# Attention on fp32 operands with one turn on TensorE, in front of two feed-forward layers: a new attention part of a fused kernel

## The chip, the cores and the metric

One Trainium2 chip, of which the kernel uses one core. The metric is the device time of one execution in microseconds (us); the kernel before takes 700.09 us (median of three executions). Engine names are those of the profile: PE is TensorE's matmul, PEld its weight load, DVE is VectorE, ACT is ScalarE, POOL is GpSimd, and SP issues nearly all transfers.

## The reference

An attention with a small learned bias on the relative position, and behind it two feed-forward layers on 1152 tokens (2 batches of 576). The feed-forward weights come as 64-bit floats and are converted on the chip.

```python
B, H, S, D = 2, 8, 576, 64
scores = np.matmul(q, k.transpose(0, 1, 3, 2)) / np.sqrt(D)
x = (log1p(abs(i - j)) / log1p(max(i, 1)))[..., None]       # one value for each pair of positions
bias = np.maximum(x @ w1 + b1, 0.0) @ w2                    # 32 hidden units, 8 heads
attn = softmax(scores + bias)                               # 1e-9 is added to each row's sum
x = np.matmul(attn, v)                                      # to (1152, 512)
x = g1(x @ moe_w_in) @ moe_w_out                            # g1(h) = h * clip(h + 3, 0, 6) / 6, 2048 hidden
out = g2(x @ moe2_w_in) @ moe2_w_out                        # g2(h) = P(h) / Q(h), a cubic over a quadratic
```

## The kernel before

The program has two parts. The **attention part** runs first, and its work is written as a list of small steps (`plan`), which are issued in the order of a table of numbers (`ORDER`). Each engine executes its own instructions strictly in that order, so the table sets both what an engine does next and what it is stuck behind. The **dense part** is a loop over 96 units of the two feed-forward layers: each unit is a matmul group `h` of 12 matmuls over 384 tokens, an elementwise chain, and a matmul group `y`; three units of the first layer are already issued inside the attention part.

The attention part works on five chunks of queries (`qc` 0 to 4): four chunks of 128 positions, each for both batches (`b` 0 and 1), and a last chunk that holds the remaining 64 positions of both. A pair of heads (`hp`) is handled together, one head on each half of the 128 partitions. A "unit" `u` is one chunk and one head, so there are 40 units, and for each unit and batch there are these steps:

- **bias**: 36 groups (`G`), eight for each of the first four chunks and four for the last. A group is four hidden-unit tiles (`bias_unit`, L528 on DVE or L526 on ACT), eight small matmuls that sum over hidden units on four column tiles of the array (`bias_sums`, L535), a scaled copy to SBUF on ACT (`bias_scaled`, L542) and a transfer that lays the rows out by position (`bias_out`, L551). `huge` holds the bias of a chunk, and there are two such buffers.
- **splitting q, k and v**: each is multiplied by a power of two and split into two fp16 parts, high and low. The power comes from sums of squares that PE takes (`gram`, L472, 128-column fp32 matmuls), that DVE turns into an exponent (L476 to L505). ACT writes the high parts (L577, L588, L597), DVE or POOL the low parts (L570, L572, L573).
- **scores**: 16 fp16 matmuls for a pair, four products of high and low parts, one head on each half of the array's rows (L613, L628 for the last chunk). They write two of the three two-bank PSUM buffers of `ps2`.
- **logits**: one DVE instruction that adds the bias and finds the row's extreme (`logits`, L636), and one that reads the accumulator. **exp** on ACT (L917).
- **turning the exponentials** so that keys lie on partitions. For 24 of the 40 units (`BY_DMA`): ACT writes a high fp16 part (L926), POOL the low part (L931), and a DMA transpose turns both (L938). For the other 16: PE turns three 128x128 blocks at a time into one PSUM bank (L950, 40 such pieces), ACT writes the high part (L957) and DVE the low part (L963). All those pieces, and the turning of the results, use one and the same bank (`pst`).
- **product with v**: 15 fp16 matmuls of 65 columns for each unit and batch (L650). The 65th column of v is ones and gives the row's sum. DVE divides (L658 to L663), PE turns the result (L670), ACT and DVE split it for the dense part (L679, L680).

SP's queue holds the loads, the bias transfers and the DMA transposes, in the table's order as well. The dense part's weights arrive as 64-bit words; DVE converts them (L213 to L215), ACT and POOL split them (L241, L242). Six of the 64 weight tiles are loaded and converted inside the attention part.

Of the kernel before, what the change touches and what calls it, by code (L numbers as in the profile page):

```python
# [10 lines left out]
F32 = mybir.dt.float32  # L11
F32R = mybir.dt.float32r
# [21 lines left out]
EXP_SHIFT = 14  # L34
E23 = float(1 << 23)
# [4 lines left out]
PRODUCTS = ((0, 0), (0, 1), (1, 0), (1, 1))  # L40
V_DVE = (0, 1, 2, 4, 7)
UNSCALED = (0, 1, 2, 3)
U_ENG = ((0, 1, 0, 1) + (0, 1, 0, 0)) * 4 + ((0, 0, 1, 0) + (0, 1, 0, 0)) * 14
BY_DMA = (1, 2, 3, 4, 6, 7, 8, 9, 11, 12, 13, 14)
PTX = (1,) * 20 + (0,) * 20
N_W = 6
M_AT = ((33.5, 34, 38.1), (34.5, 35, 38.3), (35.5, 36, 38.6))
N_EARLY = 3
ORDER = (
# [56 lines left out]
def _constants():  # L106
# [7 lines left out]
    rps = (1.0 / psi_i.astype(np.float64)).astype(np.float32)[rows[:, p // NH].T]  # L114
    msk = (np.arange(32)[None, :] // NH == (p // HID)[:, None]).astype(np.float32)
    small = np.concatenate([psq, rps, msk, np.eye(P, dtype=np.float32)], axis=1).astype(np.float32)
    return {"cpsi": psi.astype(np.float32), "csmall": np.ascontiguousarray(small)}


def _rows(ap, parts, n):  # L120
# [1017 lines left out]
```

## Time and profile before

| what | value |
|---|---|
| median of 3 executions | 700.09 us (699.69 to 701.59) |
| span of the profiled execution, first to last instruction | 698.0 us |
| PE busy in the span | 617.2 us (88%) |
| DVE busy | 522.5 us (75%) |
| ACT busy | 415.8 us (60%) |
| POOL busy | 284.8 us (41%) |

The profiled execution's own time is its span plus what lies around it; the median above lies 2.1 us over this span. Busy time is the union of the instructions' times on an engine. A matmul's row lasts until its modelled end, and the next one starts long before that, so the cost of a row of matmuls is read from start to start. An fp32 matmul leaves two records in the trace, a turn and an fp16 matmul one.

### The profile page before, as it was taken

Reading aid. Unit: us, or ns where it says so; the run is one execution under the profiler, and the core shown is the slowest. Engines: PE = TensorE matmul, PEld = TensorE weight load, DVE = VectorE, ACT = ScalarE, POOL = GpSimd, SP = SyncE. Lnnn points to the kernel's source line nnn. Section 1 sums busy time; section 2 is a strip of 40 time slices with the busy share of each in tenths; the row PEclk is TensorE's granted clock in tenths of the full one; section 3 lists DMA queues with packets and bytes.
Section 4 is the critical chain, followed back from the end, with each engine's and each line's share of the span. In section 5 each row is a group of like instructions: output and inputs, shape, how many; then the busy total and the mean of one; then the engine's idle time right before and its main releaser. Section 6 shows DMA issues by size and latency. Waiting matters only on the chain.

```text
span 698.0 us, 12904 instructions
## 1 busy us (share of the span) xinstructions
PE 617.2 (88%) x5022; PEld 524.7 (75%) x5022; DVE 522.5 (75%) x1027; ACT 415.8 (60%) x723; POOL 284.8 (41%) x248
## 2 busy tenths in 40 slices
PE   9777988687875969799899999998899789999997
PEld 8454644254553758799899999998799679999985
DVE  6558878876796852999977847989977887666674
ACT  5747786696766443454333333356788677777863
POOL 1114654363346400334323214127456855455543
PEclk9979999899997999899999999999999999999999
DMA  6655765379768403635434600333411000000011
GB/s 241 132 190 128 155 127 131 85 171 187 152 164 213 84 1 109 193 122 181 151 122 131 228 5 30 91 92 104 137 31 31 1 1 0 1 1 0 1 76 60
DMA packets 88012, 70.87 MB, mean 102 GB/s; under 512 B 58512, under 2 KB 75024, under 8 KB 87952
## 3 DMA queue, kind: packets, MB, share of 16 engines
q1 hardware_dynamic: 87952, 70.06, 36.9%
q8 instruction: 39, 0.64, 0.4%
q14 instruction: 21, 0.17, 0.1%
HBM read 41.73 MB, written 2.36 MB: 63 GB/s over the span
## 4 chain that ended last, share of the span: by engine, by line
PE 55%; DVE 19%; issue 9%; DMA 6%; POOL 5%; ACT 5%; SPq 0%; DVEq 0%; POOLq 0%; ACTq 0%
PE y L372 21%; PE h L289 21%; DVE wk L215 3%; PE h L472 3%; PE ps L535 3%; DVE big L528 3%; DVE wk L214 3%; DVE wk L213 3%; DMA huge<-wk 2%; DMA xt<-big 2%; PE ps L613 2%; PE h L950 2%; PE h L650 2%; POOL big L931 2%; DVE big L636 2%
## 5 line engine op out<-in xcount | busy, mean ns | idle before, releaser
L289 PE MATMUL h<-xt,huge 128*128 128x384 f32 x504 | 102.4, 348 | 6.7 <-DVE gl L314 2.1
L289 PEld LDWEIGHTS h<-xt,huge 128*128 128x128 f32 x504 | 93.0, 196 | 10.7 <-DVE gl L314 2.8
L324 POOL TENSOR_TENSOR e<-e,e 128x384 f32<-128x384 f32 x48 | 51.1, 1066 | 64.3 <-ACT e L322 62.5
L931 POOL TENSOR_TENSOR big<-big,big 128x1152 f16<-128x1152 f32 x24 | 58.7, 2450 | 41.4 <-ACT big L926 40.3
L636 DVE CUSTOM_DVE_ANT_0 big<-ps,huge,nscale 128x576 f32<-128x576 f32 (+1 forms) x72 | 57.3, 819 | 20.9 <-PE ps L613 10.8
L289 PE MATMUL h<-xt,big 128*128 128x384 f32 x324 | 63.2, 343 | 5.4 <-DVE e L336 5.4
L289 PEld LDWEIGHTS h<-xt,big 128*128 128x128 f32 x324 | 58.2, 192 | 7.0 <-DVE e L336 6.3
L314 POOL TENSOR_TENSOR gl<-e,gh 128x384 fp32r<-128x384 f32 x48 | 50.1, 1048 | 31.8 <-ACT gh L313 23.9
L613 PE MATMUL ps<-kT,qT 64*128 64x512 f16 (+1 forms) x512 | 45.3, 306 | 19.9 <-DVE mx L636 12.8
L917 ACT ACTIVATE big<-big,mx 128x576 f32<-128x576 f32 (+1 forms) x72 | 53.6, 772 | 13.8 <-DVE mx L636 7.8
L242 POOL TENSOR_TENSOR huge<-wk,huge 128x512 fp32r<-128x512 f32 x28 | 39.5, 1428 | 53.2 <-ACT huge L241 53.2
L289 PE MATMUL h<-xt,wp 128*128 128x384 f32 x324 | 60.9, 335 | 0.0
L289 PEld LDWEIGHTS h<-xt,wp 128*128 128x128 f32 x324 | 57.1, 188 | 1.5
L528 DVE TENSOR_SCALAR big<-psw,thr 128x576 f32<-128x576 f32 x92 | 54.8, 646 | 4.0 <-PE ps L535 3.0
L535 PE MATMUL ps<-big,wblk 128*32 128x288 f32 x576 | 52.9, 436 | 5.4 <-DVE big L528 2.1
L242 POOL TENSOR_TENSOR big<-wk,big 128x512 fp32r<-128x512 f32 x18 | 23.8, 1320 | 81.1 <-ACT big L241 67.6
L215 DVE SCALAR_TENSOR_TENSOR wk<-big,wk 128x512 int32<-128x512 int32 x64 | 55.2, 863 | 0.4
L214 DVE SCALAR_TENSOR_TENSOR wk<-big,wk 128x512 int32<-128x512 int32 x64 | 54.3, 848 | 0.9
L313 ACT ACTIVATE gh<-h 128x384 fp32r<-128x384 f32 x45 | 21.7, 490 | 52.9 <-DVE h L299 30.5
L613 PEld LDWEIGHTS <-qT 64*128 64x128 f16 x512 | 21.2, 99 | 41.6 <-issue 32.2
L213 DVE TENSOR_SCALAR wk<-big 128x512 int32<-128x512 int32 x64 | 40.2, 628 | 9.3 <-POOL huge L242 4.9
L372 PE MATMUL y<-gh,huge 128*128 128x384 f32 x176 | 45.0, 341 | 0.1
(151 smaller groups left out, 1439.5 us busy)
## 6 DMA issues: line engine op xcount, KB each, us to landing
big<-in_moe_w_in_dram SPq DMA_DIRECT2D x32, 512.0 KB, 3.7
big<-in_moe_w_out_dram SPq DMA_DIRECT2D x32, 512.0 KB, 3.6
huge<-wk SPq DMA_DIRECT2D x40, 288.0 KB, 3.8
huge<-in_k_dram SPq DMA_DIRECT2D x4, 576.0 KB, 8.5
xt<-in_v_dram SPq DMA_DIRECT2D x9, 256.0 KB, 5.9
rawq<-in_q_dram SPq DMA_DIRECT2D x4, 512.0 KB, 6.3
out_dram<-part SPq DMA_DIRECT2D x5, 256.0 KB, 2.0
out_dram<-psw SPq DMA_DIRECT2D x3, 256.0 KB, 2.1
```

Of the source, the lines that this page charges most:

```text
L213: nc.vector.tensor_scalar(wt, high, 3, 0x3FFFFFFF, op0=ALU.logical_shift_left, op1=ALU.bitwise_and)
L214: nc.vector.scalar_tensor_tensor(wt, high, -0x40000000, wt, op0=ALU.bitwise_and, op1=ALU.bitwise_or)
L215: nc.vector.scalar_tensor_tensor(wt, low, 29, wt, op0=ALU.logical_shift_right, op1=ALU.bitwise_or)
L242: nc.gpsimd.tensor_tensor(lo, wt.bitcast(F32), hi.bitcast(F32), op=ALU.subtract)
L289: nc.tensor.matmul(ps, wx[:, c, :], xx[:, c, :], start=(i == c == 0), stop=(i == 2 and c == KC - 1))
L372: nc.tensor.matmul(ys[c][d][:, :wid], lhs, rhs, start=(first and i == 0), stop=(last and i == 2))
L528: eng.tensor_scalar(dst, win, thr[:, 0, g:g + 1], 0.0, op0=ALU.subtract, op1=ALU.max)
L535: nc.tensor.matmul(ps[32 * ct:32 * ct + 32, hf, :HS], wblk.rearrange("p i h -> p (i h)"), units_of[G, ct][:, hf * HS:(hf + 1) * HS], start ...
L613: nc.tensor.matmul(ps[e][:, c0:c0 + n], x[r, i0, b, hp, :], kT[r, i1, hp, S * b + c0:S * b + c0 + n], start=(j == 0), stop=(j == len(PRODU ...
L636: nc.vector.tensor_tensor_reduce(ss, ps[:, :n], biases[qc][:, h * S:h * S + n], op0=ALU.add, op1=ALU.min, scale=nscale[:, qc:qc + 1], scal ...
L917: nc.scalar.activation(ss, ss, AF.Exp, bias=mxs[u // 2][:, b, u % 2:u % 2 + 1], scale=-1.0)
L931: nc.gpsimd.tensor_tensor(hls[u][:, 1], pes[u], hls[u][:, 0], op=ALU.subtract)
```

## The change

The attention part is written anew; the dense part's functions stay.

- q, k and v are loaded as fp32 and used as they are. The sums of squares, the powers of two, the fp16 parts and all their steps are gone. `scores` now issues four fp32 matmuls of 288 columns for a pair (row L516, L531 for the last chunk) in place of 16.
- The exponentials stay fp32. All 40 units are turned on PE, 112 pieces with 328 turns in all (L706), and each piece is copied out once, by ACT (L714) or by DVE (L716). DMA transposes, high parts and low parts are gone.
- The product with v is turned round: v is the stationary operand, the turned exponentials move, and the two heads of a pair lie on the two halves of the array's columns. That is 10 fp32 matmuls of 128 columns for a pair and batch (L551), 400 in all, 80 of them with 64 columns. The result comes out with the head's dimension on partitions, so that no result is turned.
- The rows' sums come from the exponential itself (`accum_out`). Their reciprocals are turned and spread over the partitions by PE (`recips`, `spread_rc`, L755, L771), and one DVE instruction multiplies (L778).
- One PSUM pool of four banks (`pools["h"]`) serves the bias sums, the turned pieces, the products with v, the spread reciprocals and later the dense part's `h`. `ps2` has two buffers in place of three. The bias sums of a group go to two banks, one for each half of the columns, with a copy for each.
- The tables `U_ENG`, `EV_ENG` and `OUT_ENG` say which of DVE and ACT takes each bias unit and each copy; 109 of 144 bias units go to DVE (104 before). `ORDER` is new.

```diff
-    pools["h", 0] = ctx.enter_context(tc.tile_pool(name="psh0", bufs=1, space=PSUM, reuse_waits="tile"))
+    pools = {"h": ctx.enter_context(tc.tile_pool(name="psh", bufs=4, space=PSUM, reuse_waits="tile"))}
...
-        ps2 = scores_ctx.enter_context(tc.tile_pool(name="ps2", bufs=3, space=PSUM))
+        ps2 = scores_ctx.enter_context(tc.tile_pool(name="ps2", bufs=2, space=PSUM))
...
-        def bias_sums(G):
-
-            ps = T(ps2, [P, 2, 512], F32, "ps2")
...
+        def bias_sums(G, hf):
+
+            ps = BANK()
+            for ct in range(4):
...
-            x = qts[qc].rearrange("p a (b h t) -> p a b h t", h=NPAIR, t=P)
+            x = raws[qc].rearrange("p (b h t) -> p b h t", h=NPAIR, t=P)
             if qc < 4:
-                for j, (i0, i1) in enumerate(PRODUCTS):
-                    for c0, n in ((0, 512), (512, 64)):
-                        for e, r in enumerate(rows):
-                            nc.tensor.matmul(ps[e][:, c0:c0 + n], x[r, i0, b, hp, :],
-                                             kT[r, i1, hp, S * b + c0:S * b + c0 + n], start=(j == 0),
-                                             stop=(j == len(PRODUCTS) - 1), tile_position=(64 * e, 0))
-                return ps
+                for c in range(2):
+                    for e, r in enumerate(rows):
+                        nc.tensor.matmul(ps[e][:, 512 - HS * (1 - c):512 + HS * c] if c else ps[e][:, 512 - HS:512],
+                                         x[r, b, hp, :], kraw[r, hp, S * b + HS * c:S * b + HS * c + HS],
+                                         start=True, stop=True, tile_position=(64 * e, 0))
+                return [p[:, 512 - HS:512 + HS] for p in ps]
...
-        def av(o, pt, h, b, rows, coff):
-            n = rows.stop - rows.start
-            i = 0
-            for px, vx in ((pt[:, 0], vh), (pt[:, 0], vl), (pt[:, 1], vh)):
-                for c in range(5):
-                    m = NKC if (b, c) == (1, 0) else c + 4 * b
-                    nc.tensor.matmul(o[rows, :], px[:, coff + c, rows.start:rows.start + n], vx[:, m, h, :],
-                                     start=(i == 0), stop=(i == 14), tile_position=(0, rows.start))
-                    i += 1
...
+        def av(o, pt, hp, b, cols, coff):
+            for c in range(5):
+                m = NKC if (b, c) == (1, 0) else c + 4 * b
+                for e in range(2):
+                    nc.tensor.matmul(o[64 * e:64 * e + 64], vraw[:, m, 2 * hp + e, :], pt[e][:, coff + c, cols],
+                                     start=(c == 0), stop=(c == 4), tile_position=(0, 64 * e))
...
+            nc.scalar.activation(ss, ss, AF.Exp, bias=mxs[u // 2][:, b, u % 2:u % 2 + 1], scale=-1.0,
+                                 accum_out=sums[qc][:, b, h:h + 1])
...
-            nc.scalar.activation(pts[u][:, 0, c], ps, AF.Copy, scale=2.0 ** EXP_SHIFT)
...
-            nc.vector.scalar_tensor_tensor(pts[u][:, 1, c], ps, 2.0 ** EXP_SHIFT, pts[u][:, 0, c], op0=ALU.mult, op1=ALU.subtract)
...
+            if eng is nc.scalar:
+                nc.scalar.activation(pts[u][:, c], ps, AF.Copy)
+            else:
+                nc.vector.tensor_copy(pts[u][:, c], ps)
```

The order on PE at the start of the program, before: `rawq` and `huge` in L472 are q and k, `ssq` are sums of squares, `big` a group's bias units. The second half of each group repeats the first and is left out.

```order
L728 MATMUL ps_24_120<-ones_82 128x128 x18
L472 MATMUL h_141<-rawq_139 128x128 x8
L535 MATMUL ps_30_163<-big_157,wblk_90 32x288 x2
L535 MATMUL ps_30_163<-big_160,wblk_90 32x288 x2
L535 MATMUL ps_32_176<-big_118,wblk_90 32x288 x2
L535 MATMUL ps_32_176<-big_173,wblk_90 32x288 x2
L472 MATMUL h_202<-huge_81 128x128 x27
L483 MATMUL h_236<-ssq_84,ones_82 128x1
L472 MATMUL h_202<-huge_81 128x128 x9
L483 MATMUL h_269<-ssq_84,ones_82 128x1
```

The same place now: `kraw` and `rawq` are k and q as loaded.

```order
L598 MATMUL h_91<-ones_83 128x128 x18
L484 MATMUL h_139<-big_127,wblk_89 32x288 x2
L484 MATMUL h_139<-big_129,wblk_89 32x288 x2
L484 MATMUL h_148<-big_127,wblk_89 32x288 x2
L484 MATMUL h_148<-big_129,wblk_89 32x288 x2
L516 MATMUL ps_25_155<-kraw_79,rawq_118 128x288
L516 MATMUL ps_26_156<-kraw_79,rawq_118 128x288
```

The first scores have moved up behind the first bias group; the sums of squares that stood there are gone. Thirteen more bias groups follow before the second scores.

The order on PE in the second chunk, before: a piece of three turns (L950), then ten of the 15 matmuls of a unit's product (L650, each with its own weight load, of which one pair of rows stands here), a bias group, two pieces, a bias group.

```order
L950 MATMUL h_1581<-csm_79,big_1205 128x128 x3
L650 LDWEIGHTS xt_1504
L650 MATMUL h_1470<-vh_98,xt_1504 128x65
L650 MATMUL h_1470<-vl_99,xt_1504 128x65
L535 MATMUL ps_248_1607<-big_1555,wblk_90 32x288 x2
L535 MATMUL ps_248_1607<-big_1558,wblk_90 32x288 x2
L950 MATMUL h_1628<-csm_79,big_1250 128x128 x3
L950 MATMUL h_1637<-csm_79,big_1250 128x128 x3
L535 MATMUL ps_258_1647<-big_1621,wblk_90 32x288 x2
L535 MATMUL ps_258_1647<-big_1644,wblk_90 32x288 x2
```

A like place now: six pieces of a pair of units on the four shared banks, both halves of a bias group, scores, and the product with v, whose two heads alternate.

```order
L706 MATMUL h_933<-csm_76,big_828 128x128 x3
L706 MATMUL h_941<-csm_76,big_853 128x128 x3
L706 MATMUL h_946<-csm_76,big_828 128x128 x3
L706 MATMUL h_954<-csm_76,big_828 128x128 x3
L706 MATMUL h_959<-csm_76,big_853 128x128 x3
L706 MATMUL h_965<-csm_76,big_853 128x128 x3
L484 MATMUL h_970<-big_742,wblk_89 32x288 x2
L484 MATMUL h_977<-big_742,wblk_89 32x288 x2
L516 MATMUL ps_225_984<-kraw_79,rawq_438 128x288
L516 MATMUL ps_226_985<-kraw_79,rawq_438 128x288
L551 MATMUL h_995<-xt_932,vraw_80 64x128
L551 MATMUL h_995<-xt_940,vraw_80 64x128
```

The turns and the products now hold most of PE's rows; the scores' rows have become few.

The order on SP's queue behind the first chunk's bias, before: `huge<-wk` is a bias transfer, `xt<-big` a DMA transpose.

```order
L551 DMA huge_825<-wk_717 16x8x576
L938 DMA_TRANSPOSE xt_830<-big_727 128x18x128
L938 DMA_TRANSPOSE xt_863<-big_822 128x18x128
L938 DMA_TRANSPOSE xt_925<-big_866 128x18x128
L938 DMA_TRANSPOSE xt_1012<-big_899 128x18x128
L551 DMA huge_825<-wk_869 16x8x576
```

The same stretch now:

```order
L501 DMA huge_342<-wk_543 16x8x576
L423 DMA kraw_79<-in_k_dram 128x1152
L569 DMA big_677<-in_cpsi_dram 128x640
L501 DMA huge_793<-wk_648 16x8x576
L501 DMA huge_793<-wk_754 16x8x576
```

The transposes that stood between the bias transfers are gone, and the last head pair's k is loaded here.

## Rows read from the trace of the kernel before

**Rows 1.** The page's part 2: busy tenths in 40 slices of the span.

```profile
PE   9777988687875969799899999998899789999997
...
DVE  6558878876796852999977847989977887666674
```

**Rows 2.** Busy time by stretch: start and end, length, then engines, clock, DMA share.

```profile
0.00:38.00 38.00, 28.61 (x273) 21.41 (x274) 20.12 (x53) 21.44 (x28) 6.42 (x19) 0.93 0.68 197
38.00:286.00 248.00, 195.52 (x2689) 132.44 (x2688) 181.88 (x414) 157.11 (x233) 99.01 (x77) 0.92 0.57 137
286.00:698.00 412.00, 393.04 (x2060) 370.89 (x2060) 320.50 (x562) 237.21 (x462) 179.35 (x153) 0.98 0.23 71
```

**Rows 3.** The logits (L636): count, durations in ns, first and last start.

```profile
L636 DVE CUSTOM_DVE_ANT_0 big<-ps,huge,nscale x72: 787/814/884, 38.0 to 257.2; 128x576 f32<-128x576 f32 x64, 128x640 f32<-128x640 f32 x8
```

**Rows 4.** The chain that ended last, up to 290 us: by line, and pieces.

```profile
by line: PE h L472 8.1%; PE ps L535 7.9%; issue 7.1%; DVE big L528 7.0%; DMA huge<-wk 5.5%; DMA xt<-big 4.8%; PE ps L613 4.5%; PE h L950 4.4%; PE h L650 4.3%; POOL big L931 4.1%; DVE big L636 4.1%; PE h L289 3.8%; PE y L372 2.7%; DVE wk L21
...
57.39 1.95 ACT vh L588 x3
...
69.61 1.27 POOL vl L573
...
154.34 1.99 PE h L650 x60
...
359.50 2.08 PE h L289 x12
```

**Rows 5.** Longest waits up to 286 us: total, times, longest.

```profile
ACT big L957 <- PE h L950: 30.5, 23, 4.2
DVE big L963 <- ACT big L957: 29.1, 23, 4.3
```

**Rows 6.** PE in order of time, merged: start, duration, what.

```profile
156.26 1.18 PE L535 MATMUL ps<-big,wblk 128*32 128x288 f32 x16
157.37 1.15 PE L613 MATMUL ps<-kT,qT 64*128 64x512 f16 x16
158.45 0.66 PE L670 MATMUL h<-csm,xo 128*128 128x128 f32 x4
159.04 0.39 PE L613 MATMUL ps<-kT,qT 64*128 64x512 f16 x1
```

**Rows 7.** PE in order of time, the first sums of squares of k.

```profile
11.92 6.29 PE L472 MATMUL h<-huge 128*128 128x128 f32 x54
```

**Rows 8.** Bias units on DVE: all of them by line, then in time beside POOL.

```profile
L528 DVE TENSOR_SCALAR big<-psw,thr x92: 489/515/2624, 6.3 to 175.9; 128x576 f32<-128x576 f32 x92
...
116.74 3.69 DVE L528 TENSOR_SCALAR big<-psw,thr 128x576 f32<-128x576 f32 x4
...
117.02 2.24 POOL L573 TENSOR_TENSOR qT<-rawq,qT 128x1024 f16<-128x1024 f32 x1
```

**Rows 9.** DVE and ACT groups: busy us, mean ns of one, idle before.

```profile
L528 DVE TENSOR_SCALAR big<-psw,thr 128x576 f32<-128x576 f32 x92 | 54.8, 646 | 4.0 <-PE ps L535 3.0 <-issue 0.4 <-POOL big L931 0.3
L963 DVE SCALAR_TENSOR_TENSOR big<-h,big 128x384 f16<-128x384 f32 x20 | 11.1, 556 | 20.5 <-ACT big L957 20.5
L636 DVE DVE_READ_ACCUMULATOR2_ANT mx<- 128x1 f32 x72 | 5.9, 82 | 0.0
L917 ACT ACTIVATE big<-big,mx 128x576 f32<-128x576 f32 x64 | 47.0, 766 | 12.3 <-DVE mx L636 6.3 <-POOL mx L910 6.0
L957 ACT ACTIVATE big<-h 128x384 f16<-128x384 f32 x20 | 9.8, 488 | 22.5 <-PE h L950 22.5
```

**Rows 10.** Bias transfers in the page's list: count, KB each, us to landing.

```profile
huge<-wk SPq DMA_DIRECT2D x40, 288.0 KB, 3.8
```

More of the change, by code (lines that the diff above doesn't have):

```diff
@@ L631, in scores @@
-            return ps
+            for i in range(2):
+                for b, spans in ((0, ((0, 320), (320, 256))), (1, ((64, 256), (320, 320)))):
+                    c0, n = spans[i]
+                    o = slice(64 * b, 64 * b + 64)
+                    for e, r in enumerate(rows):
+                        nc.tensor.matmul(ps[e][o, z + c0:z + c0 + n], x[r, 0, hp, o],
+                                         kraw[r, hp, c0 + 512 * b:c0 + 512 * b + n], start=True, stop=True,
+                                         tile_position=(64 * e, 64 * b))
@@ L810, in q_low @@
-        def q_low(qc):
-            need(("q high", qc))
-            prep_q_low(qc, (nc.gpsimd, nc.vector)[qc == 0])
-            done.add(("qT", qc))
-        for qc in range(5):
-            t = -4.2 if qc == 0 else 8 * qc - 6
-            at(t, q_high, qc)
-            at(t + .1, q_low, qc)
         def group_unit(G, ct, eng):
@@ L916, in unit_exp @@
+            qc, h = units[u]
+            n = S if qc < 4 else S + 64
             ss = pes[u][:, b * n:(b + 1) * n]
[L917 removed]
+            if qc not in sums:
+                sums[qc] = T(apool, [P, 2, NH], F32, "sums", bufs=3)
+            nc.scalar.activation(ss, ss, AF.Exp, bias=mxs[u // 2][:, b, u % 2:u % 2 + 1], scale=-1.0,
+                                 accum_out=sums[qc][:, b, h:h + 1])
             done.add(("e", u, b))
[L920 to L921 removed]
@@ L923, in unit_high, with n_pieces @@
[L923 to L939 removed]
+        def n_pieces(u):
+            return 3 if u < 32 else 2
@@ new lines, in pair_out, with recips @@
+        def pair_out(p, eng):
+            qc, hp = divmod(p, NPAIR)
+            need(("av", p, 0), ("av", p, 1))
+            if qc not in oT:
+                oT[qc] = T(apool, [P, 2, NPAIR, P], F32, "oT", bufs=2)
+            o, dst = os_.pop(p)[:, :nb_of(qc)], oT[qc][:, :nb_of(qc), hp]
+            if eng is nc.scalar:
+                nc.scalar.activation(dst, o, AF.Copy)
+            else:
+                nc.vector.tensor_copy(dst, o)
+            done.add(("o", p))
+        def recips(qc):
+            n = nb_of(qc)
+            need(*(("e", 8 * qc + h, b) for h in range(NH) for b in range(n)))
+            s = sums[qc][:, :n]
+            nc.vector.tensor_scalar(s, s, 1e-9, None, op0=ALU.add)
+            nc.vector.reciprocal(s, s)
+            done.add(("rc", qc))
@@ new lines, in recips_turn, with recips_out @@
+        def recips_turn(qc):
+            need(("rc", qc), "csm")
+            ps = BANK((P, KC, P))
+            for b in range(nb_of(qc)):
+                nc.tensor.matmul(ps[:NH, b], sums[qc][:, b], ident, start=True, stop=True)
+            held["rcT", qc] = ps
+            done.add(("rct", qc))
+        def recips_out(qc):
+            need(("rct", qc))
+            n = nb_of(qc)
+            t = T(apool, [NH, 2, P], F32, "rcT", bufs=2)
+            nc.scalar.activation(t[:, :n], held.pop(("rcT", qc))[:NH, :n], AF.Copy)
+            rcs[qc] = t
+            done.add(("rcs", qc))
@@ new lines, in spread_rc, with x_scaled @@
+        def spread_rc(qc, b):
+            need(("rcs", qc), "sel")
+            ps = BANK((P, KC, P))
+            for hp in range(NPAIR):
+                nc.tensor.matmul(ps[:, hp], sel[:, hp * P:(hp + 1) * P], rcs[qc][:, b], start=True, stop=True)
+            held["bc", qc, b] = ps
+            done.add(("bc", qc, b))
+        def x_scaled(qc, b):
+            need(("bc", qc, b), *(("o", 4 * qc + hp) for hp in range(NPAIR)))
+            o = oT[qc][:, b]
+            nc.vector.tensor_tensor(o, o, held.pop(("bc", qc, b)), op=ALU.mult)
+            done.add(("xs", qc, b))
@@ L1061, in fused_kernel @@
             at(30 + .7 * i, w_bits, it)
-            at(32.5 + .7 * i, w_split, it)
+            at(32.5 + .7 * i, w_high, it)
+            at(32.6 + .7 * i, w_low, it)
         def scores_done():
-            need(*(("r", u, b) for u in range(40) for b in range(len(chunks_of(units[u][0])))))
+            need("bias sums done", *(("r", u, b) for u in range(40) for b in range(len(chunks_of(units[u][0])))))
             scores_ctx.close()
@@ new lines, in step_high, with step_low @@
+        def step_high(j):
+            need(("g", j))
+            two = BIG([P, 2, TC], F32R)
+            gh_of[j] = two[:, 0], two[:, 1]
+            nc.scalar.activation(two[:, 0], held["relu", j], AF.Copy)
+            done.add(("gh", j))
+        def step_low(j):
+            need(("gh", j))
+            gh, gl = gh_of[j]
+            nc.gpsimd.tensor_tensor(gl, held.pop(("relu", j)), gh.bitcast(F32), op=ALU.subtract)
+            gi, L, g, c, f, _, _ = steps[j]
+            gs[gi, c, f] = gh, gl
+            ahead.add((mid, j))
+            done.add(("gl", j))
@@ L1084, in fused_kernel, with step_y @@
+        def step_y(j):
+            gi, L, g, c, f, _, _ = steps[j]
+            need(("gl", j), "y", ("w", items(0)[2 * f + 1]), *((("back", j - 1),) if j else ()))
+            back(*steps[j])
+            ahead.add((back, j))
+            done.add(("back", j))
         at(38, scores_done)
-        for j, ts in enumerate(M_AT):
-            for fn, t in zip((front, mid, back), ts):
-                at(t, step, fn, j)
+        for j, t in enumerate(M_AT):
+            for i, fn in enumerate((step_h, step_relu, step_g, step_high, step_low, step_y)):
+                at(t + (0, .1, .2, .3, .4, 3.6)[i], fn, j)
```

491 lines of the change are left out of this document (140 added, 351 removed), and 87 rows, old and new, of tables (EV_ENG, ORDER, U_ENG).

## The prediction

> **What bounds the kernel now.** I began with the slices [rows 1]. From the eighteenth on PE is at 8 or 9 nearly everywhere; ahead of that it is at 5 to 9, and no engine is full. So there are two kernels in one. To find the border I cut the span where PE's dense run begins, at 286 us [rows 2]: of the 412 us behind it PE is busy 393. A dense group of 12 matmuls takes 2.08 us on the chain [rows 4]; the change does not touch that loop, so I carry the 412 us over unchanged. All of the change lies in the 286 us ahead.
>
> There the logits mark the progress: the first starts at 38.0 us [rows 3]. Before it stand the sums of squares, the splitting and the first chunk's bias. In the 248 us between, PE is busy 195.5, DVE 181.9, ACT 157.1, POOL 99.0 [rows 2]. PE's figure flatters, since its rows overlap. From start to start I price a bias group at 1.11 us, a scores group at 1.08, four turns at 0.59 (0.148 each) [rows 6], an fp32 matmul of 128 columns at 0.233 (54 records, 27 matmuls, 6.29 us) [rows 7] and a matmul of the product with v at 0.033 [rows 4]. What PE does after 38 us is then 28 bias groups 31.1, 36 scores 38.9, 64 matmuls for sums of squares 14.9, 148 turns 21.9, 1200 product matmuls 39.8 and six early dense groups 12.5, together 159 us: 64% of 248. DVE is at 73%. So nobody is the bound; the engines wait for one another. The longest waits say where: ACT waits 30.5 us for turned pieces and DVE 29.1 us for ACT's high parts [rows 5], a ring of three engines round one PSUM bank. On the chain up to 290 us stand sums of squares 8.1%, DMA transposes 4.8% and POOL's low parts 4.1% [rows 4].
>
> **The change, part by part.**
>
> Start. The first bias unit starts at 6.3 us [rows 8]. In the new order 41 units stand on DVE ahead of the first logits (23 before); at the undisturbed 0.515 us [rows 8] these take 21.1 us, so the first logits come at 27.4 at the earliest. The bias itself must have landed by then: 3.8 us for each transfer [rows 10], and nothing has to be scaled first. I take 28 us. The later end is 38 us, if the transfers of the first chunk are as late as now.
>
> PE from then on. By the order, 14 bias groups are done before the second scores, so 22 remain: 22 x 1.11 = 24.4. A scores group is two fp32 matmuls of 288 columns on each half of the rows. No such row exists; an fp32 matmul of 288 columns costs 0.233 x 288/128 = 0.524 us, and the bias groups do two on each of four column tiles in 1.11 [rows 6], that is 2 x 0.524 plus 0.06, so fp32 tiles run side by side. I take the same 1.11 for two row tiles, since the fp16 scores run their two halves side by side too: 36 x 1.11 = 40.0. If the halves took turns it would be 80. The turns: 328 x 0.148 = 48.5; at the 0.117 of one record in an unmixed run [rows 7] 38.4, and I keep the higher, which contains the change of shape around them. The product: five fp32 matmuls on each of two column tiles, 5 x 0.233 = 1.17, for 32 pairs and batches, and half of it for the eight with 64 columns: 42.1 (84 if the two tiles took turns). Reciprocals: 45 matmuls x 0.233 = 10.5. Early dense groups 12.5 as before. Sum 178.0 us, 19 more than now.
>
> DVE. 68 units x 0.515 = 35.0, 72 logits with their accumulator reads x 0.896 = 64.5 [rows 3, 9], 44 copies of pieces at most 0.556 [rows 9] = 24.5 (a low part reads one tensor more), and at most 26 for products, scaling and six weight tiles: 150 us. ACT: 20 units at about 0.77 like its exponentials = 15.4, 46 half rows of bias at most 0.488 = 22.4, 72 exponentials x 0.77 = 55.4, 68 copies x 0.488 = 33.2 [rows 9], and some 17 of small work: 143. The sum that the exponential now gives may cost ACT nothing, or a read like DVE's 0.082 us [rows 9], 5.9 in all. Both stay 28 us or more under PE, so who copies what has no price of its own, as long as PE's 178 us cover it.
>
> One price of DVE's needs a second look. Four bias units took 3.69 us beside a POOL instruction of 2.24 us, where undisturbed ones take 0.515 each [rows 8]; hence the mean of 646 ns [rows 9]. POOL is busy 99 us in these stretches [rows 2], and the change leaves it a few low parts. At the mean the 68 units are 43.9 us, undisturbed 35.0. The Trainium skill (SBUF — State Buffer, "Who interferes with whom") says that VectorE and GpSimd share a pair of ports that one instruction holds whole, and names tensor_scalar among those that take it. By that rule the lower sum holds; the trace agrees with its 3.69 us. Neither makes DVE the bound.
>
> How full PE gets. 178 us at 64%, the share of now, is 278 us; at 100% it is 178. What speaks for more than 64%: the ring round one bank becomes one copy, with four banks, and the DMA transposes and POOL's low parts leave the path. In the new order pieces, bias sums and product stand between one scores group and the next, so that two logits (1.8 us) and exponentials have cover on PE. What speaks for less: four banks now serve everyone, and with two buffers of `ps2` PE can't start the next scores until both logits are done. Between the two ends, and because the waits that made the 64% are the ones removed, I take 85%, above DVE's 73% of now: 178/0.85 = 209. The attention part then ends at 28 + 209 = 237 us instead of 286, and the time is 237 + 412 + 2 (what lies around the span) = 651, rounded to 652.
>
> A second way, by the chain: 17.0% of 290 us, that is 49, goes with the three removed kinds, and 13.5 us with the splitting of v (57.4 to 70.9) [rows 4]; PE's 19 us come back. 286 - 62.8 + 19 = 242, which makes 656. The two ways share little, so I believe the size.
>
> **Rivals.**
>
> PE is fed nearly always (97%): 178/0.97 = 184, the part ends at 212, time 626. For it: no other engine has more than 150 us. Against it: no stretch ahead of 286 looks so now.
>
> Tiles of one kind take turns, either in the scores or in the product: 40 or 42 us more on PE, 219/0.85 + 28 = 286, time 700, no change. For it: neither an fp32 row tile nor an fp32 tile of 64 columns is in the trace. Against it: four fp32 column tiles overlap [rows 6].
>
> Slower: the four shared banks become the ring. Every bias half, piece, product and reciprocal asks for the bank that was taken four requests ago; where its copy stands late on DVE or ACT, PE halts with all that is queued behind, the scores too. If PE stays at 64%, 178/0.64 = 278, the part ends at 306, time 720. It decides at 178/(286 - 28) = 69%. For it: ACT and DVE wait for PE's pieces now for 30 us [rows 5], and PE has 19 us more to do. Against it: each bank is held for one copy of about 0.5 us, not two in series.
>
> The removed steps were covered anyway, and only the start gains: 10 us off by the earlier logits, 19 on by PE, time about 700 too. Against it: the chain, where they stand openly.
>
> **How the numbers follow.** The forecast (635 to 676) 0.60; PE nearly full (620 to 635) 0.15; a part-way gain (676 to 695) 0.06; no gain to speak of (695 to 705, tiles or cover) 0.08; slower by the banks 0.11. Less than 0.3%, 2.1 us, can't be told from no change. Faster takes the first three and a part of the fourth: 0.84; same 0.03; slower 0.13. The range 620 to 694 leaves out the last two cases and little else.
>
> **What would show it.** First logits near 28 us; the dense run beginning near 237; behind it 412 us again. A scores group of 8 records in 1.1 us, ten product matmuls in 1.2, bias units near 0.515 in the mean. PE waiting little for DVE and ACT copies. Wrong, if scores or products take double, if PE's waits name L714, L716 or L492 for tens of us, or if the dense run itself gets longer.

## The result, and the profile after

The changed kernel takes 627.97 us (median of four runs, 625.21 to 631.73); the kernel before took 700.8 beside it. The ratio is 0.8963, with a 95% interval of 0.8926 to 0.8999. The profiled execution took 629.39 us, of which 627.6 are its span. The forecast was 652, the range 620 to 694: faster, as said, but 24 us further, and nearly at the 626 of the rival in which PE is fed nearly always. So not the case that had been given 0.60 (635 to 676) came, but the one with 0.15 (620 to 635).

The page's slices of the changed kernel, in tenths as in [rows 1], show the difference at once. The holes of the first seventeen slices are gone: from the second slice on PE stands at 9 nearly everywhere, in the attention part as in the dense run. In the attention part, which now ends in the fourteenth slice, DVE is at 5 to 8 and ACT at 4 to 9.

```profile
PE   7999999999999999989999999988998799999996
DVE  7777678678785789987874698899678876775684
ACT  5987677878674455333433324766786777777762
PEclk9999899999998999999999999998999799999999
```

I cut the span at the first logits and at the last matmul that is not of the dense run. The columns are those of [rows 2].

```profile
0.00:28.10 28.10, 24.62 (x248) 13.87 (x252) 20.23 (x51) 20.47 (x40) 1.62 (x10) 1.00 0.76 215
28.10:206.40 178.30, 176.17 (x1964) 124.61 (x1955) 130.64 (x308) 131.80 (x311) 19.90 (x18) 0.98 0.39 106
206.40:627.60 421.20, 401.32 (x2138) 379.92 (x2136) 326.76 (x574) 241.97 (x472) 183.28 (x156) 0.99 0.24 75
```

Set beside [rows 2], the 70.4 us between the two spans are: 38.0 - 28.1 = 9.9 at the start, 248.0 - 178.3 = 69.7 in the attention part, and 421.2 - 412.0 = 9.2 given back by the dense run. The last has a plain cause: 2138 matmuls stand behind the cut where 2060 stood, and 78 at the 0.173 us of [rows 4] (2.08/12) are 13.5 us. They are dense groups that the kernel before did ahead of the cut. That is 4 us more than the 9.2, so the same dense work got a little quicker; the section on the prediction comes back to it.

In the middle stretch PE is busy 176.2 of 178.3 us. Busy rows of PE flatter, as the prediction says, so I took the starts: PE in order of time (start, duration, what) in a steady piece of the stretch. A row begins shortly before the one ahead of it ends.

```profile
83.78 2.02 PE L706 MATMUL h<-csm,big 128*128 128x128 f32 x17
85.73 1.18 PE L484 MATMUL h<-big,wblk 128*32 128x288 f32 x16
86.83 1.31 PE L551 MATMUL h<-xt,vraw 128*64 128x128 f32 x20
88.08 1.24 PE L516 MATMUL ps<-kraw,rawq 64*128 64x288 f32 x8
89.25 1.31 PE L551 MATMUL h<-xt,vraw 128*64 128x128 f32 x20
90.49 1.18 PE L484 MATMUL h<-big,wblk 128*32 128x288 f32 x16
```

From start to start these are 17 turns in 1.95 us (0.115 each), sixteen bias records in 1.10, ten product matmuls (two records each) in 1.25, and a scores group in 1.17. No idle time is between them. The waits of the stretch say the same from the other side: DVE and ACT now wait mostly for PE. (Who waited, for whom: us in total, times, longest; POOL's waits, up to 126.6 us for the little that it has to do, are left out.)

```profile
DVE big L539 <- PE ps L516: 18.3, 21, 2.5
...
ACT big L714 <- PE h L706: 12.2, 9, 3.6
ACT big L690 <- DVE mx L539: 8.5, 7, 1.6
...
ACT xt L714 <- PE h L706: 6.9, 11, 1.7
...
PE h L706 <- ACT wk L492: 1.1, 1, 1.1
```

The waits of [rows 5], 30.5 us of ACT for pieces and 29.1 of DVE for ACT, have no counterpart of that size, and PE's own longest is 1.1 us. By line, the chain that ended last in this stretch is PE's (the first entries of its row are L551 21.7%, L706 19.4%, L516 18.5%, L484 13.5%).

### The profile page after: what moved, and what is told of

Same layout as the page of the kernel before. It is cut to its first block, busy times and chain, and to the rows that moved or that the text cites. A ratio compares the mean times of both kernels' runs of the same rounds, so it can differ in the third digit from the quotient of the medians.

```text
span 627.6 us, 11425 instructions
## 1 busy us (share of the span) xinstructions
PE 602.1 (96%) x4342; PEld 518.4 (83%) x4342; DVE 477.6 (76%) x933; ACT 394.2 (63%) x822; POOL 204.8 (33%) x183
## 4 chain that ended last, share of the span: by engine, by line
PE 70%; DVE 13%; issue 7%; DMA 4%; ACT 3%; POOL 2%; SPq 1%; DVEq 0%; POOLq 0%; ACTq 0%
PE h L290 23%; PE y L373 22%; PE h L551 6%; PE h L706 6%; PE ps L516 5%; PE h L484 5%; DVE wk L219 3%; DVE wk L218 3%; DVE wk L220 3%; PE h L771 1%; DMA huge<-wk 1%; DMA kraw<-in_k_dram 1%; DMA bcoef<-in_moe_b_dram 1%; POOL big L247 1%; ACT wk L492 1%
## 5 line engine op out<-in xcount | busy, mean ns | idle before, releaser
L290 PE MATMUL h<-xt,huge 128*128 128x384 f32 x504 | 99.2, 339 | 3.1 <-DVE e L337 3.1
L539 DVE CUSTOM_DVE_ANT_0 big<-ps,huge 128x576 f32<-128x576 f32 (+1 forms) x72 | 53.1, 760 | 26.5 <-PE ps L516 18.3
L219 DVE SCALAR_TENSOR_TENSOR wk<-big,wk 128x512 int32<-128x512 int32 x64 | 55.3, 864 | 0.8
L797 POOL TENSOR_TENSOR xt<-oT,xt 128x512 fp32r<-128x512 f32 x8 | 10.2, 1275 | 126.7 <-ACT xt L791 126.6
L220 DVE SCALAR_TENSOR_TENSOR wk<-big,wk 128x512 int32<-128x512 int32 x64 | 49.7, 777 | 0.4
L484 PE MATMUL h<-big,wblk 128*32 128x288 f32 x576 | 47.0, 413 | 1.3 <-ACT wk L492 1.3
L706 PE MATMUL h<-csm,big 128*128 128x128 f32 x328 | 46.7, 285 | 1.1 <-ACT wk L492 1.1
L706 PEld LDWEIGHTS h<-csm,big 128*128 128x128 f32 x328 | 35.7, 144 | 14.2 <-issue 6.9
L478 DVE TENSOR_SCALAR big<-psw,thr 128x576 f32<-128x576 f32 x99 | 44.6, 513 | 1.4 <-PE h L484 1.3
L247 POOL TENSOR_TENSOR huge<-wk,huge 128x512 fp32r<-128x512 f32 x24 | 34.5, 1458 | 26.2 <-ACT huge L246 26.2
L326 DVE TENSOR_TENSOR e<-e,h 128x384 f32<-128x384 f32 x48 | 26.3, 548 | 21.7 <-ACT e L324 21.6
```

The source lines that it names most:

```text
L219: nc.vector.scalar_tensor_tensor(wt, high, -0x40000000, wt, op0=ALU.bitwise_and, op1=ALU.bitwise_or)
L220: nc.vector.scalar_tensor_tensor(wt, low, 29, wt, op0=ALU.logical_shift_right, op1=ALU.bitwise_or)
L290: nc.tensor.matmul(ps, wx[:, c, :], xx[:, c, :], start=(i == c == 0), stop=(i == 2 and c == KC - 1))
L478: eng.tensor_scalar(dst, win, thr[:, 1, g:g + 1], 0.0, op0=ALU.add, op1=ALU.max)
L484: nc.tensor.matmul(ps[32 * ct:32 * ct + 32, :HS], wblk.rearrange("p i h -> p (i h)"), units_of[G, ct][:, hf * HS:(hf + 1) * HS], start=Tru ...
L539: nc.vector.tensor_tensor_reduce(ss, ps, biases[qc][:, h * S:h * S + n], op0=ALU.add, op1=ALU.min, scale=-0.125, scalar=3e38, accum_out=mx)
```

## The experiments

Twelve kernels ran, all variants of the changed one. To compare them I use two figures of each profile: when the first logits start, and the stretch from there to the last matmul ahead of the pure dense run. The changed kernel has 28.1 and 178.3 us.

### What fills PE: the order of the work

```
-ORDER = (0, 24, 1, 25, 2, 3, 26, 27, 4, 21, ...)
+ORDER = ()
```

> The changed kernel with its table of order emptied, so that the pieces of work are issued in the plain order of their due times. Theory 1 (it is the order that keeps PE full, 176.8 of 178.9 us between the first logits and the dense run): PE waits for copies again, its share in the attention part falls towards 80%, the part gets 172/0.80 - 179 = 36 us longer, the time about 664 us; at the 64% of the kernel before it would be 717. Rival (shorter rings, one copy for each piece and four banks, keep PE full in any order): at most 10 us more, 628 to 638.

Measured: 724.33 us, ratio 1.0355 (1.0301 to 1.0408). With every other part of the change in place the kernel is slower than the one before. The first logits come at 30.0, the stretch is 283.2 us. What PE does in it is the changed kernel's work plus 48 early dense matmuls: (178.3 - 2.1 + 8.3)/283.2 = 65%, where 2.1 is PE's idle time in the changed kernel's stretch. That is nearly the 64% of the kernel before, but by another loss: no ring round one bank is left, and what PE waits for most is bias units. Theory 1 holds, and its size was not the 664 us for 80% but the other end that it named, 717 at 64%, and a little past it. PE in order of time shows how it is lost (in brackets idle time and what ended it):

```profile
83.64 0.67 PE L443 MATMUL h<-big,wblk 128*32 128x288 f32 x2 [0.28 <-DVE big L437]
84.53 0.67 PE L443 MATMUL h<-big,wblk 128*32 128x288 f32 x2 [0.22 <-DVE big L437]
85.64 0.67 PE L443 MATMUL h<-big,wblk 128*32 128x288 f32 x2 [0.43 <-DVE big L437]
...
87.05 0.69 PE L443 MATMUL h<-big,wblk 128*32 128x288 f32 x8
87.67 1.24 PE L475 MATMUL ps<-kraw,rawq 64*128 64x288 f32 x8
...
94.69 2.40 PE L510 MATMUL h<-xt,vraw 128*64 128x128 f32 x40
```

and in the waits:

```profile
PEld h L443 <- DVE big L437: 40.4, 42, 3.4
...
PE h L443 <- DVE big L437: 22.3, 35, 2.9
```

The bias sums (L443 here; L437 is the bias units, L475 the scores) come two records at a time, each pair as DVE delivers one unit. The idle time in brackets understates the loss, since a pair alone lasts 0.67 us, and where the units were ready eight such records took 0.62 us from start to start (87.05 to 87.67). The next run moves the units alone.

```
+LEAD = 1.0
...
 ORDER = ()
...
-                at(t + .15 * ct, group_unit, G, ct, ...)
+                at(t + .15 * ct - LEAD, group_unit, G, ct, ...)
```

> The plain order of due times again, but every bias unit is due one period (1.0) earlier, so that the units of the next group stand ahead of the sums of this one. In the plain order PE's bias sums took 74.6 us for 446 records where the changed kernel's price of 0.074 each makes 32.9, with 26.4 us of idle time ahead of them: 68 us. Theory 1a (PE halts there because a sum stands right behind its units): most of the 68 us come back, 656 to 680 us. Rival 1b (the plain order loses at many places, and the wait only moves to pieces and products): 700 us or more.

Measured: 683.96 us, 0.9756 (0.9723 to 0.9789); first logits 25.7, stretch 239.9. Of the 105 us that the plain order costs in the stretch, 43 come back, 40 us of the whole time. The time lies 4 us beyond theory 1a's range and 16 short of 1b's: the missing lead of the bias units is 43 of the 105 us, not the 68 that theory 1a counted on. A part of what remains can be read in PE's rows: the scores (L476) wait for the logits (L499) to free their banks, and behind that the clock falls. The last line is the window of the product (L511) with PE, PEld, DVE, ACT and POOL, clock and DMA as in [rows 2].

```profile
88.76 0.72 PE L476 MATMUL ps<-kraw,rawq 64*128 64x288 f32 x2 [0.41 <-DVE mx L499]
90.76 1.20 PE L476 MATMUL ps<-kraw,rawq 64*128 64x288 f32 x6 [1.28 <-DVE mx L499]
91.89 4.07 PE L511 MATMUL h<-xt,vraw 128*64 128x128 f32 x40
...
91.90:95.90 4.00, 4.00 (x42) 3.83 (x41) 0.52 (x2) 0.00 (x0) 0.00 (x0) 0.57 0.11 38
```

The granted clock is 0.57 from 91.9 to 95.9 us, nearly the lower level of 1.2 GHz, behind these two halts; forty product records took 4.07 us, where the same forty took 2.40 in the plain order without the lead. Over the stretch both runs have a clock of 0.93, the changed kernel 0.98: a part of the order's gain is clock, how much no run tells.

### How many shared banks it takes

```
-    pools = {"h": ...tile_pool(name="psh", bufs=4, space=PSUM, ...)}
+    pools = {"h": ...tile_pool(name="psh", bufs=3, space=PSUM, ...),
+             "h2": ...tile_pool(name="psh2", bufs=1, space=PSUM, ...)}
+    n_h = [0]
...
-        ps = BANK()[:, :TC]
+        n_h[0] += 1
+        own = n_h[0] <= N_EARLY or n_h[0] % 4 >= 3
+        ps = T(pools["h2" if own else "h"], [P, 512], F32, "h")[:, :TC]
```

This is the edit for three banks, in `h_unit` the dense groups' part of it; for two, both pools have two buffers and the 3 is a 2.

> Attention has three shared PSUM banks in place of four; the dense run keeps its four (the fourth bank serves it alone). Theory 1 (the order leaves each copy time enough): little is lost, 628 to 634 us. Rival 2 (the four banks make the fill): PE halts about once in each scores period for a copy of 0.5 us, 36 x 0.5 = 18 us, 646 us or more.

> Attention has two shared PSUM banks in place of four; the dense run keeps its four. Both theories expect a loss, of different size. Theory 1 (order first): a copy of 0.5 us and its hand-over stand open at a part of the 188 uses, 20 to 40 us, 648 to 668 us, and less than the loss without the table of order. Rival 2 (the banks make the fill): the loss is larger than that without the table of order, PE at 64 to 70%, about 700 us.

Three banks: 634.68 us, 0.9063 (0.9021 to 0.9105), stretch 182.0. Two banks: 664.39 us, 0.9471 (0.9409 to 0.9533), stretch 215.9. So the fourth bank is worth 4 us of the stretch and the third 34. Two banks lie in theory 1's range, three 0.7 us beyond it. PE's waits for copies do come back, but only at two banks, in small bites (L710 is the turns, L488 the bias sums, L718 and L496 their copies on ACT):

```profile
PEld h L710 <- ACT xt L718: 7.5, 16, 1.0
...
PEld h L710 <- ACT big L718: 6.7, 11, 1.7
PEld h L488 <- ACT wk L496: 6.7, 11, 1.7
```

The Trainium skill (Perfetto Trace Analysis, "Matmuls" under "Optimizing Tensor Performance") advises that independent matmul groups rotate through different PSUM banks so that their evacuation overlaps the next group. The runs agree, and put the price on it: 34 us from two banks to three, then 4. Even two banks with the order beat four without it, 215.9 against 283.2 us. The order is the one used with four banks in all three; one laid out for two or three did not run.

### Who copies the pieces

```
-EV_ENG = (1, 1, 1, 1, 0, 1, 1, ...)
+EV_ENG = (0,) * 120
```

The second of the two runs has `(1,) * 120` there.

> All 112 copies of turned pieces on DVE (44 before this edit): DVE +68 x 0.556 = 37.8 us, so 169 of the 179 us in the attention part; ACT loses 33. Theory 1 (PE is the bound and the others have cover): PE's wait stays small, 628 to 640 us. Rival 3 (the table of order places each copy for its engine, so a copy that queues behind two logits of 0.84 us holds its bank and PE with it): 650 to 670 us.

> All 112 copies of turned pieces on ACT (68 before this edit): ACT +44 x 0.49 = 21.6 us, 153 of the 179 us in the attention part; DVE loses 24. Theory 1 (PE is the bound, and a copy on the other engine costs only where it stands behind a long instruction): as with all copies on DVE, about 10 us or less, 628 to 640. Rival 3 (the engine of each copy matters as much as its place in the order): 645 or more.

On DVE: 640.23 us, 0.9134 (0.91 to 0.9169), stretch 187.6, DVE at 158.5 of it. On ACT: 630.41 us, 0.8984 (0.8944 to 0.9024), stretch 182.6. The first lies 0.2 us over theory 1's upper edge and is clear of the changed kernel's time; the second lies near the lower edge and can't be told from it. So "who copies what has no price of its own" was right within 4 us of the stretch for ACT and 9 for DVE (12 of the time). On DVE the copies stand ahead of logits: ACT then waits 46.3 us for DVE's maxima (8.5 in the changed kernel), and most of that is still covered.

```profile
ACT big L687 <- DVE mx L536: 46.3, 41, 3.6
```

### Whether PE is the bound, from above and from below

More work, first in the product: the same matmuls, one column tile after the other.

```
-            for c in range(5):
-                m = NKC if (b, c) == (1, 0) else c + 4 * b
-                for e in range(2):
+            for e in range(2):
+                for c in range(5):
+                    m = NKC if (b, c) == (1, 0) else c + 4 * b
                     nc.tensor.matmul(o[64 * e:64 * e + 64], vraw[:, m, 2 * hp + e, :], pt[e][:, coff + c, cols],
```

> The product with v issues its five matmuls of one column tile, then the five of the other, where the changed kernel alternates between the two tiles. Same matmuls, same result. If the two tiles run side by side when they alternate, ten matmuls take 5 slots; one tile after the other they take 9 to 10, and PE's 46.2 us for the product grow by 37 to 46. Theory 1 (tiles overlap and PE is the bound): 665 to 674 us. Rival (tiles take turns in any order): 628. Rival (they overlap, but PE has hidden slack): growth of PE's busy time without that of the span, below 650.

Measured: 655.22 us, 0.935 (0.9303 to 0.9397), stretch 202.2, PE idle 1.8 us of it. Ten matmuls now take 1.95 us from start to start, where the changed kernel alternates in 1.25:

```profile
41.17 2.02 PE L551 MATMUL h<-xt,vraw 128*64 128x128 f32 x20 [0.61 <-ACT wk L492]
43.12 1.24 PE L516 MATMUL ps<-kraw,rawq 64*128 64x288 f32 x8
```

So fp32 tiles on two column halves run side by side here when they alternate. The product's sum over all records rose by 25.2 us (46.2 to 71.4) and not by 37 or more: if five slots take 1.25 us, ten matmuls in this order take 1.95/0.25 = 7.8 slots and not the nine or ten that were expected. So the time ends 10 us short of theory 1's range, and above the 650 of the rival with hidden slack; the stretch rose by 23.9, that is 95% of PE's added work. Next, the turns twice:

```
+for _ in range(2):
     nc.tensor.transpose(ps[:, c - c0], pes[u][:, c * P:(c + 1) * P], ident)
```

> Each matmul that turns a piece is issued twice into the same place (328 more, same result). Theory 1 (PE is the bound, nothing else): 328 x 0.109 = 36 us at the start-to-start time of one in a row, so 664 us. Rival (waits of the pieces' copies set the pace, so more work on PE partly falls into them): less than half, below 646 us.

Measured: 658.45 us, 0.9392 (0.9356 to 0.9429), 5.5 short of theory 1's 664 and far above the rival's 646; stretch 208.1: 29.8 us more, and PE idle 0.3. The turns' sum grew by 34.6 us (43.5 to 78.1), and about 2 us of PE's idle time and some of what the other groups had lost were used up. Added work on PE thus costs 86 to 95% of itself. Taking work away:

```
-        wblk = T(apool, [P, 4, NH], F32, "wblk")
+        wblk = T(apool, [P, 4, NH], F16, "wblk")
...
-                two = BIG([P, 2, S], F32)
+                two = BIG([P, 2, S], F16)
```

> The bias units and their weights are rounded to fp16, so that the bias sums are fp16 matmuls; nothing else changes. A group of 16 took 1.11 us in fp32 and should take about a quarter to a half, so that PE loses 20 us of its 27.4 after the first logits. Theory 1 (PE is the bound down to DVE's and ACT's 131 us): 605 to 612 us, with the first logits little earlier, since DVE's units set that. Rival (copies and logits bound the pace right behind PE): PE idles instead, 620 to 628 us.

Measured: 619.64 us, 0.8847 (0.8803 to 0.8891). The time lies between the two ranges, 0.4 us short of the rival's. The bias sums fell from 27.3 to 10.0 us, the stretch by 13.2 to 165.1; PE idles 4.9 us, and the clock is 0.97. (The columns are those of [rows 2]: ahead of the first logits, then the stretch.)

```profile
0.00:28.90 28.90, 20.32 (x149) 10.73 (x149) 20.23 (x51) 20.72 (x41) 1.62 (x10) 0.74 0.77 211
28.90:194.00 165.10, 160.16 (x1775) 119.54 (x1770) 130.10 (x308) 130.14 (x310) 19.99 (x18) 0.97 0.42 114
```

So 13 of the 17 us that PE saved came back, three quarters: mostly theory 1, with a quarter lost to the rival's idling. The first logits came at 28.9, 0.8 us later and not a little earlier. The last run goes further:

```
+id16 = T(apool, [P, P], F16, "id16")
...
+nc.vector.tensor_copy(id16, ident)
...
-nc.scalar.activation(ss, ss, AF.Exp, ...)
+nc.scalar.activation(pes[u].bitcast(F16)[:, b * n:(b + 1) * n], ss, AF.Exp, ...)
...
-nc.tensor.transpose(ps[:, c - c0], pes[u][...], ident)
+nc.tensor.matmul(ps[:, c - c0], pes[u].bitcast(F16)[...], id16, start=True, stop=True)
...
+at(39, lambda: nc.scalar.activation(babs, bcoef, AF.Abs))
+order = [*order, len(plan) - 1]
...
-nc.scalar.activation(babs, bcoef, AF.Abs)
```

> As the run with fp16 bias units and weights, and beside it two edits: the exponentials are written as fp16 and turned by fp16 matmuls, and a two-element activation that waits for a late parameter transfer is moved from ACT's seventh place to the end of its attention part. Bias and exponentials are then rounded to fp16, the sums are still taken in fp32. PE loses about half of its 43.7 us for the turns, so its work behind the first logits falls from 160 to 138 us, DVE and ACT stay at 130. Theory 1 (the engine with the most work sets the part, whoever it is): 140 to 148 us behind the first logits. Rival (under about 160 us copies and logits are on the path whatever PE does): 155 to 165. Start: if ACT's chain of units and scaled sums sets the first logits, they come 2 us earlier, at 26 to 27; if transfers set them, at 28 to 29. Time by theory 1 590 to 600 us, by the rival 605 to 618.

Measured: 603.7 us, 0.8621 (0.8582 to 0.8659), the fastest of all, at the price of a bias and exponentials in fp16. The windows from 0 to the first logits and over the stretch:

```profile
0.00:26.20 26.20, 18.58 (x152) 9.98 (x153) 20.40 (x53) 20.66 (x40) 1.62 (x10) 0.80 0.86 234
26.20:183.00 156.80, 149.00 (x1771) 107.90 (x1767) 128.67 (x309) 128.53 (x310) 20.11 (x18) 0.95 0.45 120
```

The turns fell from 43.7 to 28.0 us, by less than half, and the stretch by 8.3: half of that came back. A part of the rest went to PE's other groups, which took 4.6 us longer than with fp16 bias sums alone (scores 46.7 against 44.5, bias sums 11.8 against 10.0). Here the rival's range for the stretch held (155 to 165), and theory 1 (140 to 148) did not; the time ends 1.3 us below the rival's 605 to 618. While PE is a third ahead (176 us against 132) added work costs nearly all of itself; from 176 to 160 three quarters of what a group saves come back, from 160 downward, against 130, half. With PE at 149 and DVE and ACT at 128.7 and 128.5 the hand-overs begin to show, and the granted clock is 0.95 in place of 0.98.

### The start

DVE's 41 units were to set it. First their neighbour on POOL:

```
...
+for _ in range(60):
+    nc.gpsimd.tensor_tensor(scr, scr, scr, op=ALU.add)
```

> POOL gets 60 additions of 128 x 512 fp32 on a scratch tile at the start, over 60 us of work beside the bias units; no result uses them. Theory (POOL's work slows DVE's bias units, as the kernel before showed with 3.69 us for four beside one POOL instruction of 2.24): the units' mean rises from 0.514 to 0.7 or more, the first logits come 6 to 14 us later, and the time is 636 to 655 us. Rival (the slow units before had another cause): units stay at 0.515, first logits at 28 us, time 628.

Measured: 662.38 us, 0.9454 (0.9413 to 0.9495). The first logits come at 58.7, and the stretch behind them is 180.4, hardly longer. The theory is right and its size was too small. By line (durations in ns, least, median, most):

```profile
L438 POOL TENSOR_TENSOR scr<-scr x60: 1039/1134/1597, 2.8 to 74.1; 128x512 f32<-128x512 f32 x60
```

```profile
L482 DVE TENSOR_SCALAR big<-psw,thr x99: 429/1054/1294, 9.1 to 151.3; 128x576 f32<-128x576 f32 x99
```

The additions come every (74.1 - 2.8)/59 = 1.21 us, and the first 41 units every (57.5 - 9.1)/40 = 1.21 too: one of the one, one of the other. The Trainium skill (SBUF — State Buffer, "Who interferes with whom") says that, of GpSimd and a VectorE instruction in a two-port mode, whoever issues first gets the shared pair of ports for its whole instruction and the other blocks fully; the trace agrees with its equal 1.21 us, though no row names the units' mode. Then the units themselves, from a source of two bytes:

```
+psih = T(apool, [P, W2], F16, "psih")
...
-nc.vector.tensor_scalar(psiw, psiw, sgn, None, op0=ALU.mult)
+nc.vector.tensor_scalar(psih, psiw, sgn, None, op0=ALU.mult)
...
-win = psiw[:, S - r:2 * S - r] if G < 32 else ...
+win = psih[:, S - r:2 * S - r] if G < 32 else ...
```

> As the run with fp16 bias units and weights, with the table of log distances in fp16 too (for the first 32 groups), so that DVE and ACT read 2 bytes an element. The bias is then rounded at its input as well; nothing else changes. Theory 2a (DVE takes less time for a unit whose source and result are 2 bytes wide, down to half of 0.514 us): 41 units ahead of the first logits take 11 to 16 us in place of 21, the first logits come at 18 to 24 us, DVE loses a further 10 us or so behind them, and the time is 602 to 614 us. Rival 2b (a unit costs its 576 elements whatever the width, as with the fp16 result alone): 615 to 622.

Measured: 620.62 us, 0.8852 (0.8813 to 0.889): no gain over fp16 sums alone. A unit does get cheaper,

```profile
L479 DVE TENSOR_SCALAR big<-psih,thr x99: 277/364/1037, 6.0 to 111.2; 128x576 f16<-128x576 f16 x99
```

0.364 us in place of 0.514, but the first logits stay at 28.7, and so the time lies in rival 2b's range without 2b's reason. Theory 2a is right that a unit gets cheaper and wrong on the consequence: DVE does not set the start. Nor does it set the stretch: DVE's work there fell from 130.1 to 121.7 us, and the stretch is 166.8 us against 165.1. At the start ACT is what is late: in the changed kernel it waits, behind four bias units, for a parameter of two columns (L926), with the first scaled bias sums (L492) queued behind, and from there it is busy on end up to the logits.

```profile
6.43 2.78 ACT L476 ACTIVATE big<-psw,thr 128x576 f32<-128x576 f32 x4 [4.41 <-DVE psw L632]
11.69 0.20 ACT L926 ACTIVATE babs<-bcoef 128x2 f32<-128x2 f32 x1 [2.47 <-DMA bcoef<-in_moe_b_dram]
11.80 0.48 ACT L492 ACTIVATE wk<-h,csm 128x288 f32<-128x288 f32 x1
```

With that one instruction moved, in the run with fp16 exponentials, the first logits came at 26.2, as expected if ACT's chain sets them, against 28.9 with the fp16 bias sums alone: 2.7 us for a wait that was 3.15 us long there (2.47 in the changed kernel). The fp16 exponentials of the same run act behind the first logits, save for a copy of the identity.

## Why the prediction was right, and where its sizes were off

**PE's work: right.** Summed over the stretch from each record's start to the next one's (idle time left out): 369 bias records 27.3 us (predicted 24.4), scores 43.2 (40.0), 328 turns 43.5 (48.5), product 46.2 (42.1), reciprocals and their spreading 11.3 (10.5), early dense matmuls 4.8 (12.5). Together 176.3, against 178.0. That the sums agree to 1% is partly luck: the other terms are off by 8 to 12% to either side, the dense ones by more than half, and the errors cancel. The mechanism holds, since the bounds with tiles that take turns (80 and 84 us) are out. DVE came to 130.6 (150), ACT to 131.8 (143), though the sum that the exponential gives costs ACT a read of 0.196 us in the mean, 14.1 in all, where I had allowed 0 to 5.9.

**How full PE gets: the term that was mis-sized.** "Between the two ends ... I take 85%": it was 176.2/178.3, 98.8%, so that the stretch took 178 us where 209 stood in the sum. That is 30.7 us too many. The reason given for 85, that the waits that made the 64% are the ones removed, was not enough by itself: with the same single copies and the same four banks, but in plain order, PE falls to 65% and the kernel to 724 us. The order, of which the prediction said one sentence, is worth 105 us of the stretch, more than the 70 that the change gained there. The second way, by the chain (656), missed by as much on the same side, so its agreement with the first proved nothing: neither has a term for the new order. The fourth bank is worth 4 us of it, the third 34 more, and the choice of the copies' engines 4 to 9. What the removal of the old steps is worth by itself stays open: no run puts them back under the new order, and none gives the kernel before, which has an order table of its own, another order.

**The dense run: 412 carried over, 421.2 measured.** It begins at 206.4, not at 237, with 24 dense matmuls done. The prediction's 12.5 us stand for 72, and the 412 us for the 100 that the kernel before had done by 286 us; the six groups were a misreading, since 100 matmuls are more than eight. The two errors nearly cancel (7.7 us less of PE's work in the stretch, 9.2 more behind it). So the sign "if the dense run itself gets longer" did come, by matmuls that moved there and not by a slower loop.

**The start: right for a wrong reason.** 28.1 was measured, 28 predicted. But 41 units do not take 0.515 each: they follow one another at 17.70/41 = 0.432 us and end at 24.1, and DVE then waits 4.0 us.

```profile
6.44 17.70 DVE L478 TENSOR_SCALAR big<-psw,thr 128x576 f32<-128x576 f32 x41
28.15 0.76 DVE L539 CUSTOM_DVE_ANT_0 big<-ps,huge 128x576 f32<-128x576 f32 x1 [4.01 <-PE h L484]
```

That quicker units leave the first logits in place, and a removed wait of ACT's moves them, shows that ACT's chain and what follows it end last there; the units set it only where they were slowed to one in 1.21 us. The units came undisturbed, as the prediction took them: 0.513 in the mean against the 0.646 of [rows 9]. The prediction's start has no term for ACT's chain, and the 28 us that came out right are luck.

With the measured terms the sum is 28.1 + 178.3 + 421.2 + 1.8 = 629.4, the profiled execution.

**The rivals.** PE nearly full was the case (626 given, 15% chance); the range was right because it took in this rival, 8 us above its lower end. That the four banks become the ring did not happen; two banks cost 36 us of the time, and even that ends below 700. That tiles take turns was wrong, and the run that issues one half after the other shows what that costs in the product: 27 us, not 42. "Only the start gains" is out: the stretch alone gained 70 us, the start 10.

What stays open: behind its 97th matmul the dense run took 408.7 us, and 414.8 in the kernel before; that code is unchanged, and the granted clock is 0.99 against 0.98. In the twelve variants the same work took 406.1 to 411.1 us, so the one profile of the kernel before lies 3.7 us outside their spread; no run isolates why. Why the plain order with a lead still loses 62 us of the stretch is read from its waits and clock, not taken apart by a further run.

## What to carry to other kernels

Price the engine that will have the most work from start to start, and ask separately how full the order lets it be: here nearly the same work on the same banks took 178 or 283 us by order alone, and one thing to look for is an instruction whose input is made just ahead of it on another engine. A fill that is taken over from the old schedule tells little about a new one; bound it by both ends, and let the order rows (how much independent work stands between producer and consumer) choose between them. And a number that comes out right is no proof of its step: check which engine waits just ahead of the mark.

## What the runs showed of the hardware that was not expected

An fp32 turn of 128 columns took 0.109 us from start to start within a piece, half of an fp32 matmul of that size (0.233 by [rows 7]); the fp16 matmul in its place 0.056 at best and 0.085 in the mean of all 328, idle time left out. DVE's bias unit took 0.514 us with an fp16 result from an fp32 source, no less than in fp32, and 0.364 only when the source had two bytes as well. With the fp16 bias sums the granted clock ahead of the first logits was 0.74 in place of 1.00, with PE busy for 20.3 us there in place of 24.6.
